# A retention state product on four 64x64 tiles of TensorE

## The chip, the cores and the metric

One core of a Trainium2 chip. The metric is the device time of one execution in microseconds; the verdict on a difference of 2% uses fast runs alone. The rounds ran on several chips, so each ratio is to the kernel before in the same rounds.

PE is TensorE, which multiplies matrices; DVE is VectorE, ACT is ScalarE, POOL is GpSimd; PEld is PE's loading of weights. PSUM is the memory that PE writes its products to. In the views, sps are the scores, ops the outputs (of the state product and of scores times values), xT the outputs times the decays, nps the tokens' product, ld the loaded q, k and v. A tile mode is the way in which the array is divided, as 64*64; a drain is here the time from the start of a group's last record to the start of the next group's first one in another mode.

## The reference, cut to what matters

Retention with a decay per head, then a mixture of experts in which each token runs one expert. The change lies in the first half; the second sees it only through the order of the 512 features.

```python
B, H, S, DH = 8, 8, 576, 64
gamma = 1.0 - 2.0 ** (-5.0 - arange(H))
ret = (q @ k.T / 8) * where(i >= j, gamma ** (i - j), 0)    # per head
x = (ret @ v) -> (B, S, H * DH)
# experts: fresh expert = argmax(x @ w_gate), kept from the token before where
# sigmoid(x @ w_local) >= 0.5; out = softmax prob * relu(x @ w1[e]) @ w2[e]
```

## The kernel before: the parts that matter

The 4608 tokens are cut into 36 chunks of 128. A sum of k-times-v per head (`kv`) carries the past from chunk to chunk. Two heads are stacked on the 128 partitions, so ACT copies `kv` into a block-diagonal `states`: head 2c in the upper left 64x64 block, head 2c+1 in the lower right, zeros elsewhere. One matmul then serves two heads.

```python
ps_s = pool(part, "ps_s", 3, PSUM)      # scores
ps_o = pool(part, "ps_o", 2, PSUM)      # outputs
ps_n = pool(part, "ps_n", 1, PSUM)      # outputs by token, two banks
ps_kv = pool(part, "ps_kv", 1, PSUM)
...
def outputs(i):                                          # cut
    ops = ps_o.tile([P, HP, P], F32, name="ops")
    if m > 0:                                            # the state product
        n = HALF if m == MID else P
        for c in range(HP):
            nc.tensor.matmul(ops[:, c, 0:n], lhsT=states[(i + 1) % 2][:, c, :], rhs=qT[:, c, 0:n], ...)
    if m != PER - 1:
        ...                                              # kv += k.T v, 8 matmuls on 128x64 tiles
        for u in range(2):
            nc.scalar.copy(states[i % 2][half(u), :, half(u)], kv[half(u)])
    for c in range(HP):                                  # scores times values, 128x64 tiles
        for u in range(2):
            nc.tensor.matmul(ops[half(u), c, :], lhsT=vs[...], rhs=sT[:, u, c, :], ...)
    nc.vector.tensor_tensor(xT, ops, decq[:, :, at:at + P], op=Alu.mult)
...
scores(0)
for i in range(NCH + 1):
    if i + 1 < NCH: scores(i + 1)        # 8 matmuls, 64x128 tiles
    if i < NCH: outputs(i)
    if i > 0: by_token(i - 1)            # 4 matmuls, whole array
```

A sequence has 576 tokens, so a pair of sequences is 9 chunks: the first has no past, the middle one (m = 4) ends one sequence and begins the next and streams only 64 columns in the state product.

## Time and profile before

| | before |
|---|---|
| median of the first three runs | 843.18 us |
| retention half, to the start of the last tokens' product | 177.70 us |
| one normal chunk on PE | 4.80 us |
| of it, state product to the start of kv | 1.09 us |

Two groups of the page's list of the costliest ones, the state product and the copies of the state. The columns are line, engine, operation, output and inputs, shapes and count, then busy time and mean ns of one, then idle time before.

```profile
L152 PE MATMUL ops<-ld,state 128*128 128x128 f32 (+1 forms) x256 | 36.7, 286 | 0.0
...
L167 ACT COPY state<-kv 64x256 f32<-64x256 f32 x64 | 23.5, 367 | 77.3 <-PE kv L162 76.5
```

The first has no idle time before it: PE goes from group to group. The second is on an engine that waits for PE. The 286 ns are the modelled length of one pipelined record, not its price: 36.7 us over 256 records is 143 ns.

### The profile page before, as it was taken

The numbers are of one execution on the slowest core, as the hardware profiler recorded it, in microseconds if no ns is written. First come the engines' busy times: TensorE is split into PE (matmuls) and PEld (weight loads), VectorE is DVE, ScalarE is ACT, GpSimd is POOL, SyncE is SP. The second block draws the span as 40 slices with busy tenths as digits, with TensorE's granted clock in tenths as the row PEclk, the third lists the DMA queues.
The fourth block names the chain that finished last, engine by engine and source line by source line (L and its number), as shares of the span: only waits on it lengthen the run. The fifth ranks groups of instructions, "written<-read, shape, count | busy, mean of one in ns | idle before, by whom it ended". The sixth has DMA issues, their size and how long they took to land.

```text
span 840.0 us, 10642 instructions
## 1 busy us (share of the span) xinstructions
PE 760.1 (90%) x4158; PEld 497.6 (59%) x4158; DVE 171.1 (20%) x314; ACT 99.8 (12%) x230; POOL 139.3 (17%) x157
## 2 busy tenths in 40 slices
PE   6999999951699999999799979998999999999991
PEld 5888888841556654754375456547544754565460
DVE  3444545458302021002101100210021011100000
ACT  1222222210011100110011001001100100011010
POOL 7322222210433021103101110210001001100000
PEclk9999999985799999999899999999999999999996
DMA  9788888616733321512420142213303301200000
GB/s 361 268 286 276 296 273 289 228 51 228 263 111 104 102 65 46 179 56 89 145 102 27 63 147 101 65 47 124 114 13 135 115 14 59 109 14 11 27 28 5
DMA packets 27649, 105.77 MB, mean 126 GB/s; under 512 B 4607, under 2 KB 4607, under 8 KB 22785
## 3 DMA queue, kind: packets, MB, share of 16 engines
q1 hardware_dynamic: 19584, 80.75, 27.6%
q0 software_dynamic: 7120, 22.03, 7.8%
q8 instruction: 71, 1.16, 0.6%
q10 hardware_dynamic: 816, 1.37, 0.4%
q14 instruction: 58, 0.47, 0.2%
HBM read 85.25 MB, written 20.19 MB: 126 GB/s over the span
## 4 chain that ended last, share of the span: by engine, by line
issue 49%; DMA 23%; PE 19%; POOL 4%; DVE 1%; POOLq 1%; SPq 0%; ACT 0%; ACTq 0%; another core or an unknown queue 0%; DVEq 0%
DMA out_dram<-y,sidx 19%; PE nps L183 5%; PE sps L133 4%; PE ops L152 4%; PE ops L171 4%; POOL xg L430 3%; DMA w2s<-in_w_dram 2%; PE kv L162 2%; DMA decq<-in_decay_q_dram 2%; POOL out_dram L470 0%; SPq L424 0%; POOLq L470 0%; POOLq L477 0%; POOLq L481 0%; ACT x L186 0%
## 5 line engine op out<-in xcount | busy, mean ns | idle before, releaser
L466 PE MATMUL yps<-w2s,hT 128*128 128x512 f32 x656 | 285.8, 593 | 0.6 <-PEq L477 0.6
L410 PE MATMUL hps<-xTs,w1s 128*128 128x384 f32 (+4 forms) x1024 | 265.5, 422 | 16.2 <-issue 15.3
L410 PEld LDWEIGHTS hps<-xTs,w1s 128*128 128x128 f32 x1024 | 189.3, 196 | 95.1 <-issue 26.1
L466 PEld LDWEIGHTS yps<-w2s,hT 128*128 128x128 f32 x656 | 123.5, 190 | 148.9 <-issue 147.4
L469 DVE TENSOR_SCALAR y<-yps,pslot 128x512 f32<-128x512 f32 x41 | 30.8, 751 | 465.9 <-PE yps L466 465.9
L412 ACT ACTIVATE hT<-hps 128x384 f32<-128x384 f32 (+4 forms) x128 | 53.5, 418 | 573.9 <-PE hps L410 515.2
L470 POOL DMA_INDIRECT out_dram<-y,sidx x41 | 40.8, 995 | 332.9 <-DVE y L469 290.5
L430 POOL DMA_INDIRECT xg<-xd,gidx x48 | 46.2, 962 | 223.0 <-PE xgps L435 169.0
L127 POOL TENSOR_TENSOR vs<-ld,deck 128x512 f32<-128x512 f32 x36 | 37.5, 1044 | 113.3 <-DMA ld<-in_qkv_dram 73.3
L133 PE MATMUL sps<-ld 64*128 64x128 f32 x576 | 44.4, 294 | 6.7 <-DMA ld<-in_qkv_dram 6.7
L137 DVE TENSOR_TENSOR sT<-sps,mask 128x512 f32<-128x512 f32 x72 | 46.4, 686 | 16.5 <-PE sps L133 16.5
L436 DVE COPY xTs<-xgps 128x512 f32<-128x512 f32 x48 | 31.6, 687 | 76.3 <-PE xgps L435 71.8
L183 PE MATMUL nps<-gates,xT 128*128 128x137 f32 x288 | 43.4, 292 | 1.1 <-DVE lt L187 0.9
L133 PEld LDWEIGHTS sps<-ld 64*128 64x128 f32 x576 | 37.3, 195 | 11.7 <-DMA ld<-in_qkv_dram 7.0
L435 PE MATMUL xgps<-ident,xg 128*128 128x128 f32 x192 | 30.8, 294 | 12.2 <-DMA xg<-xd,gidx 7.0
L183 PEld LDWEIGHTS nps<-gates,xT 128*128 128x128 f32 x288 | 36.1, 189 | 7.4 <-issue 5.3
L171 PE MATMUL ops<-sT,vs 128*64 128x128 f32 x576 | 38.9, 278 | 0.0
L435 PEld LDWEIGHTS xgps<-ident,xg 128*128 128x128 f32 x192 | 22.3, 147 | 25.8 <-issue 14.1
L152 PE MATMUL ops<-ld,state 128*128 128x128 f32 (+1 forms) x256 | 36.7, 286 | 0.0
L176 DVE TENSOR_TENSOR xT<-ops,decq 128x512 f32<-128x512 f32 x36 | 24.9, 691 | 44.9 <-PE ops L171 39.9
L152 PEld LDWEIGHTS ops<-ld,state 128*128 128x128 f32 x256 | 31.0, 191 | 3.8
L167 ACT COPY state<-kv 64x256 f32<-64x256 f32 x64 | 23.5, 367 | 77.3 <-PE kv L162 76.5
(121 smaller groups left out, 177.1 us busy)
## 6 DMA issues: line engine op xcount, KB each, us to landing
ld<-in_qkv_dram SPq DMA_DIRECT2D x36, 1024.0 KB, 6.9
w1s<-in_w_dram SPq DMA_DIRECT2D x32, 512.0 KB, 6.7
w2s<-in_w_dram SPq DMA_DIRECT2D x32, 512.0 KB, 7.9
xd<-x SPq DMA_DIRECT2D x36, 256.0 KB, 4.6
decq<-in_decay_q_dram ACTq DMA_DIRECT2D x1, 1280.0 KB
xg<-xd,gidx POOLq DMA_INDIRECT x48
out_dram<-y,sidx POOLq DMA_INDIRECT x41
deck<-in_decay_k_dram ACTq DMA_DIRECT2D x1, 36.0 KB
```

Of the source, the lines that this page charges most:

```text
L127: nc.gpsimd.tensor_tensor(vs.rearrange("p (h d) -> p h d", h=H), vn.rearrange("p (h d) -> p h d", h=H), deck[:, m, :].unsqueeze(2).to_broa ...
L133: nc.tensor.matmul(sps[u][:, c, :], lhsT=kT[half(u), c, :], rhs=qT[half(u), c, :], start=True, stop=True, skip_group_check=True)
L137: nc.vector.tensor_tensor(sT[:, u], sps[u], (mask2 if m == MID else mask).unsqueeze(1).to_broadcast([P, HP, P]), op=Alu.mult)
L152: nc.tensor.matmul(ops[:, c, 0:n], lhsT=states[(i + 1) % 2][:, c, :], rhs=qT[:, c, 0:n], start=(c == 0), stop=False, skip_group_check=True)
L171: nc.tensor.matmul(ops[half(u), c, :], lhsT=vs[:, h * DH:(h + 1) * DH], rhs=sT[:, u, c, :], start=(m == 0 and c == 0), stop=True, skip_gro ...
L183: nc.tensor.matmul(nps[:, c, 0:P + E + 1], lhsT=xT[:, c, :], rhs=gates[:, c, :], start=True, stop=True, skip_group_check=True)
L410: nc.tensor.matmul(hps[:, 0:n], lhsT=w1s[:, m, c, :], rhs=xT[:, c, base:base + n], start=(c == 0), stop=(c == DK - 1))
L412: nc.scalar.activation(hT[:, m, base:base + n], hps[:, 0:n], Act.Relu)
L430: nc.gpsimd.indirect_dma_start(out=xg, out_offset=None, in_=xd, in_offset=bass.IndirectOffsetOnAxis(ap=gidx[:, s:s + 1], axis=0))
L435: nc.tensor.transpose(xps[:, c, :], xg[:, c * P:(c + 1) * P], ident)
L466: nc.tensor.matmul(yps, lhsT=hT[:, m, u * P:(u + 1) * P], rhs=w2s[:, m, :], start=(m == 0), stop=(m == FK - 1))
L470: nc.gpsimd.indirect_dma_start(out=out, out_offset=bass.IndirectOffsetOnAxis(ap=sidx[:, s:s + 1], axis=0), in_=y, in_offset=None, bounds_c ...
```

## The change

Leave the zeros out: eight 64x64 matmuls (two row halves u times two column halves v of the array, twice) instead of four 128x128. So that all four tiles have work, each row half brings its output to both partition halves, and the heads come out in another order (`head_at`), and x's feature blocks are permuted; the host permutes the rows of the gates and of w1 alike. Row halves write different PSUM banks, so the outputs take two half-used banks, and the pool goes from two buffers to one.

```diff
+def head_at(k, u, v):
+    return 2 * (2 * k + (u ^ v)) + u
-        ps_o = pool(part, "ps_o", 2, PSUM)
+        ps_o = pool(part, "ps_o", 1, PSUM)
-        states = [once.tile([P, HP, P], F32, name=f"state{i}") for i in range(2)]
-        for t in states:
-            nc.vector.memset(t, 0.0)
+        states = [once.tile([P, HP, DH], F32, name=f"state{i}") for i in range(2)]
-            ops = ps_o.tile([P, HP, P], F32, name="ops")
+            ops = ps_o.tile([P, 2, 4 * P], F32, name="ops")
+            def place(k, u, v):
+                return ops[half(v), u, k * P:(k + 1) * P]
+            tiles = [(k, u, v) for k in range(HP // 2) for u in range(2) for v in range(2)]
-                for c in range(HP):
-                    nc.tensor.matmul(ops[:, c, 0:n], lhsT=states[(i + 1) % 2][:, c, :],
-                                     rhs=qT[:, c, 0:n], start=(c == 0), stop=False,
+                for k, u, v in tiles:
+                    c = head_at(k, u, v) // 2
+                    nc.tensor.matmul(place(k, u, v)[:, 0:n], lhsT=states[(i + 1) % 2][half(u), c, :],
+                                     rhs=qT[half(u), c, 0:n], start=(k == 0), stop=False,
-                for u in range(2):
-                    nc.scalar.copy(states[i % 2][half(u), :, half(u)], kv[half(u)])
+                nc.scalar.copy(states[i % 2], kv)
 ... (scores times values go over the same tiles; xT reads both banks;
      the decays, the gates and w1 are permuted on the host)
```

More of the change, by code (lines that the diff above doesn't have):

```diff
@@ L165, in outputs @@
                                          skip_group_check=True)
-                for u in range(2):
-                    nc.scalar.copy(states[i % 2][half(u), :, half(u)], kv[half(u)])
-            for c in range(HP):
-                for u in range(2):
-                    h = 2 * c + u
-                    nc.tensor.matmul(ops[half(u), c, :], lhsT=vs[:, h * DH:(h + 1) * DH],
-                                     rhs=sT[:, u, c, :], start=(m == 0 and c == 0), stop=True,
-                                     skip_group_check=True)
+                nc.scalar.copy(states[i % 2], kv)
+            for k, u, v in tiles:
+                h = head_at(k, u, v)
+                nc.tensor.matmul(place(k, u, v), lhsT=vs[:, h * DH:(h + 1) * DH],
+                                 rhs=sT[:, u, h // 2, :], start=(m == 0 and k == 0), stop=True,
+                                 skip_group_check=True)
             g["xT"] = xT = work.tile([P, HP, P], F32, name="xT")
             at = (m * P) % S
-            nc.vector.tensor_tensor(xT, ops, decq[:, :, at:at + P], op=Alu.mult)
+            nc.vector.tensor_tensor(
+                xT.rearrange("p (u k) s -> p u k s", u=2),
+                ops[:, :, 0:2 * P].rearrange("p u (k s) -> p u k s", k=2),
+                decq[:, :, at:at + P].rearrange("p (u k) s -> p u k s", u=2), op=Alu.mult)
         def by_token(i):
@@ L512, in _by_feature, with _heads @@
     return x.transpose(0, 3, 2, 1).reshape(NCH, P, D)
+def _heads(np):
+    return np.array([[head_at(k, u, v) for v in range(2)] for u in range(2) for k in range(HP // 2)])
 def _decays(np):
@@ L521, in _decays @@
     at = (np.arange(S + HALF) % S).astype(np.float64)
-    head = 2 * np.arange(HP)[None, :] + np.arange(P)[:, None] // DH
+    head = _heads(np)[None, :, :].repeat(DH, 0).transpose(2, 0, 1).reshape(P, HP)
     q = gamma[head][:, :, None] ** at / math.sqrt(DH)
@@ L534 @@
     i = {n: _np.asarray(a) for n, a in inputs.items()}
-    gates = _np.concatenate([i["moe_w_gate"], i["moe_w_local"]], 1)
+    order = (_heads(_np).reshape(H, 1) * DH + _np.arange(DH)).reshape(D)
+    gates = _np.concatenate([i["moe_w_gate"], i["moe_w_local"]], 1)[order]
     decay_k, decay_q = _decays(_np)
@@ L543 @@
         "wgl": gates.reshape(DK, P, E + 1).transpose(1, 0, 2).reshape(P, DK * (E + 1)),
-        "w1": i["moe_w1"].reshape(E, DK, P, FK, P).transpose(0, 2, 3, 1, 4).reshape(E, P, FK * D),
+        "w1": i["moe_w1"][:, order].reshape(E, DK, P, FK, P).transpose(0, 2, 3, 1, 4).reshape(E, P, FK * D),
         "w2": i["moe_w2"].reshape(E, FK, P, D).transpose(0, 2, 1, 3).reshape(E, P, FK * D),
```

## The prediction

> **What bounds the kernel now.** I read the page's slices first, then the busy times of two stretches, then one chunk in order of time, then the start, then single records where a merged line was too coarse. From the page, the slices:
>
> ```profile
> PE   6999999951699999999799979998999999999991
> PEclk9999999985799999999899999999999999999996
> DMA  9788888616733321512420142213303301200000
> ```
>
> One slice is 21 us. The retention half is the first eight slices and a bit, to about 178 us: PE full, its clock full, DMA high too. Then comes the routing (slices 8 to 10, PE half idle), then the experts, to 840. The diff touches the second and third parts only by permuting rows of the gates and of the first weights: same shapes, same counts, so I leave their 660 us as they are, and the question is what the 178 us become. The busy times of two stretches:
>
> ```profile
> 84.00:105.00 21.00, 21.00 (x268) 18.55 (x264) 10.50 (x20) 5.27 (x12) 5.06 (x5) 1.00 0.87 296
> 105.00:126.00 21.00, 21.00 (x291) 18.55 (x290) 9.08 (x17) 6.01 (x14) 4.34 (x5) 1.00 0.81 273
> ```
>
> PE is busy for all 21.00 us of both (columns: PE, weight loads, DVE, ACT, POOL, clock, DMA share, GB/s). DVE is at half, ACT and POOL at a quarter. DMA at 0.81 to 0.87 is the only other resource near its end. In the waits of 60 to 160 us no PE matmul waits for anything. So each chunk costs what its PE work costs. One chunk on PE, with DVE's product that reads the outputs:
>
> ```profile
> 106.57 1.21 PE L183 MATMUL nps<-gates,xT 128*128 128x137 f32 x8
> 107.70 1.16 PE L133 MATMUL sps<-ld 64*128 64x128 f32 x16
> 108.80 1.16 PE L152 MATMUL ops<-ld,state 128*128 128x128 f32 x8
> 109.88 0.69 PE L162 MATMUL kv<-vs,ld 128*64 128x64 f32 x16
> 110.40 1.04 PE L171 MATMUL ops<-sT,vs 128*64 128x128 f32 x16
> 111.37 0.38 PE L183 MATMUL nps<-gates,xT 128*128 128x137 f32 x1
> ...
> 106.69 0.69 DVE L176 TENSOR_TENSOR xT<-ops,decq 128x512 f32<-128x512 f32 x1 [1.31 <-PE ops L171]
> ```
>
> From start to start: tokens 1.13, scores 1.10, state product 1.08 to 1.09, kv 0.51 to 0.52, scores times values 0.97; sum 4.80 us per chunk. The state product is 23% of it, and half of what it multiplies is the zeros of the block-diagonal state. Each fp32 matmul leaves two records (four matmuls, x8). The start of the kernel:
>
> ```profile
> 15.32 1.16 PE L152 MATMUL ops<-ld,state 128*128 128x128 f32 x8
> 16.41 0.69 PE L162 MATMUL kv<-vs,ld 128*64 128x64 f32 x16
> 16.92 1.05 PE L171 MATMUL ops<-sT,vs 128*64 128x128 f32 x16
> 18.16 1.09 PE L183 MATMUL nps<-gates,xT 128*128 128x137 f32 x7 [0.19 <-DVE xT L176]
> ...
> 17.41 0.69 DVE L176 TENSOR_TENSOR xT<-ops,decq 128x512 f32<-128x512 f32 x1 [5.07 <-DMA decq<-in_decay_q_dram]
> ```
>
> The first xT waits 5.07 us for the decays' DMA. Meanwhile PE does all of chunk 1's outputs (15.32 to about 18.0), which it can because the outputs' PSUM tile has two buffers.
>
> **What the Trainium skill says.** (1) "TensorEngine Tiling (Array Packing)", Tiling Modes, Key Properties: tiles of one mode load weights and multiply in parallel; changing the mode drains the array. The trace agrees. Inside a two-tile group the records start in pairs 6.5 ns apart, one pair per 109 ns (scores times values, 64 columns of weights, 128 streamed) or 58 ns (kv, 64 streamed). From the last record of a group to the first of the next mode there are 201 to 205 ns (149 after 64 streamed columns); from kv to scores times values, one mode, there are only 52. (2) The same page, Restrictions and Gotchas, Gotcha 1: different row tiles must write different PSUM banks. That is why the new output tile spans two banks, half used, and has to give up its second buffer (3 + 2 + 2 + 1 banks = 8). (3) "TensorE: Matmul & The Clock Gate", LDWEIGHTS: the time of a weight load goes with its columns, not its rows. Agreed: after a drain the second load begins when the first stream ends (106 ns), and its matmul starts 107 ns later with 128 columns (state, scores), 54 ns later with 64 (kv and scores times values in the middle chunk, first gaps 107 and 160 ns).
>
> **The state product as it is.** Single records of one chunk: starts at 103.989 and 104.202 (first gap 213 ns), then 6 steps of 111.7, last at 104.872, and kv begins at 105.077 (drain 205): 213 + 670 + 205 = 1,088 ns.
>
> **The state product as it will be.** Eight matmuls 64x64, so 16 records, on four tiles, four per tile. In the order of the loop, four neighbours fall on four different tiles. If all four run together: first gap 160 (106 + 54, 64 columns of weights), two more steps of 109 (the two-tile pitch) = 218, stagger of the four about 20 (3 x 6.5), drain 204: about 602 ns. The mode changes on both sides stay two, as they are now. Saved: 1,088 - 602 = 486 ns.
>
> **The middle chunk of every pair of sequences** (4 chunks) streams only 64 columns: now 1.035 us (113.602 to 114.637, eight loads of 128 columns at 112 ns). New: first gap 107, two steps of 58, stagger 20 = 243, and then kv, which in this chunk is already in 64x64 tiles, follows with no drain, one step later (58) and without its own slow first gap (saves about 50). So about 0.30 - 0.05 = 0.25 us; saved 0.78.
>
> **The other parts.** Scores times values keep 16 records, alternate column halves as before, only the heads are in another order: 0. ACT's two copies of 64x256 (0.37 us each) become one of 128x256: ACT gains 0.37 us per chunk, but it already ends 2.2 us before the next state product: 0. The two memsets of the states (DVE, at 1.0 us) go: 0, nothing waited. The xT product reads 512 elements per partition as before, out of two banks: 0.69 us still.
>
> **The lost buffer.** The next outputs may start only when xT has read the last ones. In the steady state xT starts 0.12 us after the tokens' matmuls begin and takes 0.69, so it ends at +0.81; the next state product starts at +2.22 (1.13 + 1.10). Slack 1.4 us: no wait. At the start it does cost: chunk 1's state product must wait for xT of chunk 0, which ends at 18.10, so state, kv and scores times values (0.60 + 0.52 + 0.97 = 2.09) come after 18.15, and the first tokens' product moves from 18.16 to about 20.24. Loss 2.1 us, once; chunk 1's own saving is in that number.
>
> **Sum.** 36 chunks; 4 first ones have no state, chunk 1 is counted in the loss, 4 are middle ones, so 27 normal ones remain. 27 x 0.486 = 13.1; 4 x 0.78 = 3.1; minus 2.1: 14.1 us. 843.2 - 14.1 = 829.1 us, 1.7% less. A normal chunk becomes 4.80 - 0.49 = 4.31 us.
>
> **Rivals.**
> - DMA takes over. A chunk moves 1.00 MB in and 0.25 MB out, 1.31 million bytes. The two stretches gave 296/0.87 = 340 and 273/0.81 = 337 GB/s per full share, so a chunk can't take under about 3.9 us (estimate). At 4.31 us the share would be 0.93 on average. For it: that is close, and 2-KB packets of the stores mix in. Against it: a load issued at 101.04 landed at 108.10 and its scores ran at 112.51, 4.4 us later; with shorter chunks some 3.5 us are left. If landing slipped behind PE all the same, chunks of 4.5 us would leave 6 to 8 us of gain: 835 to 837. I give it one in ten.
> - The four tiles don't run four at a time, only two. Then 8 pairs: 160 + 6 x 109 + 204 + 10, about 1.03 us, no gain in the normal chunk, and the start's loss stays: 842 to 845. Against it: row pairs (scores) and column pairs (the values' product) both run together in this trace[...]. At 8.77 to 9.36 us, when one row tile waited for a PSUM buffer, three records of the other tile ran ahead of it, so a tile doesn't hold up its neighbour. One in fifteen.
> - The start loses nothing, because the instructions are scheduled otherwise (kv of chunk 1 needs no output buffer and could go into the wait): up to 2 us more gain, 827.
> - The lost buffer stalls every chunk. The slack of 1.4 us speaks against it; if the stall ate half of the saving, 836. Unlikely.
> - Finer overlap of four tiles, with a pitch of 100 instead of 109 or a shorter first gap: 30 to 50 ns per chunk, 1 to 1.5 us, 828.
>
> **Range and chances.** The centre is 829.1. The threshold of 2% is 826.3: it takes a group of about 0.52 us or less with the loss as told, or both a free start and a slightly faster group: 10%. Slower by over 2% needs a stall that I don't see: 1%. The rest, 89%, lies within 2%. Range of eight in ten: 826 to 834, wider upwards for DMA and for part-way concurrency.
>
> **What would show it.** In the changed profile: the state product's group with x16 records of 64*64, 0.60 us from its start to kv's; starts in fours some 6.5 ns apart; the chunk's period 4.31 us; DMA share in the stretches 0.90 to 0.95 with PE still at 21.00 of 21.00; the first tokens' product at 20.2 us, after an idle time of nearly 2.9 us ended by DVE's xT; the routing and the experts shifted by 14 us and not otherwise changed. Wrong would be: starts in twos, PE idle before the scores (loads late), PE idle before each state product (buffer), or an expert half that itself changes its time, of which nothing here speaks.

## The result, and the profile after

The changed kernel took 831.53 us (median of 4, 830.27 to 832.81), the kernel before 843.79 in the same session (median of 4). The ratio is 0.9855, 95% interval 0.9833 to 0.9876: 1.5% less, within 2%. Ratios here are the mean time of one kernel's fast runs over that of the other's in the same rounds, so not quite the ratio of the medians. The predicted 829.1 was 2.4 us too low, inside its range.

The slices of the page after (one is 20.7 us here):

```profile
PEclk9999999957799999999899989998999999999996
DMA  8899999419632122420422142233103302200000
```

DMA is now at nine tenths in the retention half. Two stretches of it (columns as before):

```profile
63.00:84.00 21.00, 21.00 (x356) 18.11 (x353) 10.51 (x21) 4.79 (x10) 5.16 (x6) 1.00 0.91 309
84.00:105.00 21.00, 21.00 (x346) 18.18 (x344) 11.28 (x21) 4.51 (x10) 5.60 (x6) 1.00 0.96 326
```

PE is still busy for all 21.00 us: DMA at 0.91 to 0.96 has not yet become the bound. One normal chunk and the first half of a middle one, PE in order of time:

```profile
103.53 0.67 PE L163 MATMUL ops<-ld,state 64*64 64x128 f32 x16
104.13 0.69 PE L173 MATMUL kv<-vs,ld 128*64 128x64 f32 x16
104.64 1.04 PE L180 MATMUL ops<-sT,vs 128*64 128x128 f32 x16
105.62 1.21 PE L195 MATMUL nps<-gates,xT 128*128 128x137 f32 x8
106.75 1.16 PE L137 MATMUL sps<-ld 64*128 64x128 f32 x16
107.84 0.46 PE L163 MATMUL ops<-ld,state 64*64 64x64 f32 x16
108.14 0.63 PE L173 MATMUL kv<-vs,ld 64*64 64x64 f32 x16
```

Read the starts: the state product has 0.60 us to kv's start where it had 1.09, and 0.30 us in the middle chunk, where it had 1.035. From state product to state product (103.53 to 107.84) a chunk takes 4.31 us. The single records of the first group start at 103.528, .535, .541, .548, then at .688, .797 and .906 for the next fours: four at a time, 6.5 ns apart, first gap 160, steps of 109. Now the start:

```profile
17.29 0.69 DVE L185 TENSOR_TENSOR xT<-ops,decq 128x512 f32<-128x512 f32 x1 [5.07 <-DMA decq<-in_decay_q_dram]
...
18.13 0.67 PE L163 MATMUL ops<-ld,state 64*64 64x128 f32 x16 [3.78 <-DVE xT L185]
...
18.73 0.84 PE L173 MATMUL kv<-vs,ld 128*64 128x64 f32 x16
...
19.35 1.92 PE L180 MATMUL ops<-sT,vs 128*64 128x128 f32 x16
...
21.20 1.83 PE L195 MATMUL nps<-gates,xT 128*128 128x137 f32 x8
```

PE waits 3.78 us for DVE's xT, as the lost buffer makes it. And then scores times values (19.35 to 21.20) take 1.85 us, not 0.97, and the tokens (21.20 to 22.96) 1.76, not 1.13. The trace's clock records say why: from 19.10 to 22.51 us PE was granted half its clock. The kernel before had a full clock from 14.4 us to the end of its retention half. So the start cost 3.04 us up to the tokens' product (18.16 to 21.20) and 0.63 in it: 3.7 us where 2.1 were expected.

From the first tokens' product to the last, 159.54 us became 143.97, that is 15.6 us less; with the 0.6 us of the slow clock taken out, 16.2, the sum of the prediction's two terms (13.1 + 3.1). The retention half ends 12.5 us earlier (177.70 to 165.17). Routing and experts together took 662.3 us before and 663.4 after. In all kernels they took 661.2 to 667.4 us, scattered over kernels whose second half is the same.

### The profile page after: what moved, and what is told of

It reads as the page before. It is cut to its first block, busy times and chain, and to the rows that moved or that the text cites. A ratio compares the mean times of both kernels' runs of the same rounds, so it can differ in the third digit from the quotient of the medians.

```text
span 828.6 us, 11144 instructions
## 1 busy us (share of the span) xinstructions
PE 744.2 (90%) x4414; PEld 481.3 (58%) x4414; DVE 170.1 (21%) x312; ACT 88.2 (11%) x198; POOL 139.4 (17%) x157
## 4 chain that ended last, share of the span: by engine, by line
issue 47%; DMA 24%; PE 21%; POOL 2%; DVE 2%; POOLq 1%; SPq 0%; ACT 0%; ACTq 0%; DVEq 0%
DMA out_dram<-y,sidx 20%; PE nps L195 5%; PE sps L137 4%; PE ops L180 4%; PE hps L422 3%; DMA w2s<-in_w_dram 2%; PE kv L173 2%; PE ops L163 2%; DMA decq<-in_decay_q_dram 2%; POOL xg L442 2%; PE xgps L447 1%; DMA xg<-xd,gidx 0%; PE yps L478 0%; SPq L436 0%; POOLq L482 0%
## 5 line engine op out<-in xcount | busy, mean ns | idle before, releaser
L137 PEld LDWEIGHTS sps<-ld 64*128 64x128 f32 x576 | 37.1, 195 | 11.4 <-DMA ld<-in_qkv_dram 6.9
L180 PEld LDWEIGHTS ops<-sT,vs 128*64 128x64 f32 x576 | 31.7, 140 | 1.0 <-issue 0.7
L198 ACT COPY x<-nps 128x512 f32<-128x512 f32 x36 | 21.1, 586 | 64.9 <-PE nps L195 64.9
L393 PE MATMUL slots<-col,row 128*128 128x156 f32 x72 | 11.4, 326 | 17.1 <-DVE col L384 17.1
```

The lines of the kernel that those rows point to most:

```text
L137: nc.tensor.matmul(sps[u][:, c, :], lhsT=kT[half(u), c, :], rhs=qT[half(u), c, :], start=True, stop=True, skip_group_check=True)
L180: nc.tensor.matmul(place(k, u, v), lhsT=vs[:, h * DH:(h + 1) * DH], rhs=sT[:, u, h // 2, :], start=(m == 0 and k == 0), stop=True, skip_gr ...
```

## The experiments

All ten gave correct results.

**1. Keep PE busy in the wait.** Is it the idle time that costs the clock? Thirteen matmuls without use go into the free tokens' tile ahead of chunk 1's outputs.

```diff
+            if i == 1:
+                warm = ps_n.tile([P, DK, 2 * P], F32, name="warm", tag="n")
+                for c in range(13):
+                    nc.tensor.matmul(warm[:, c % DK, 0:P], lhsT=gates[:, c % DK, 0:P], rhs=gates[:, 0, 0:P], ...)
```

> The changed kernel with 13 idle-time matmuls into the free tokens' PSUM tile, placed between chunk 2's scores and chunk 1's state product, about 2.9 us of work in the 3.8 us in which PE waits for the first xT. The wait itself stays. Theory 'the idle PE loses its clock': no half-clock stretch after 19 us, chunk 1's kv and scores times values at 0.52 and 0.98 us instead of 0.62 and 1.85, first tokens' product at 20.2 us instead of 21.2, end of the retention half 1.6 us earlier than in the changed kernel (last tokens' product at about 163.6 instead of 165.2). Rival 'the slow stretch has another cause (loads, PSUM)': it stays, first tokens' product at 21.2 or later.

PE at the start:

```profile
15.34 3.17 PE L211 MATMUL warm<-gates 128*128 128x128 f32 x26
18.55 0.67 PE L164 MATMUL ops<-ld,state 64*64 64x128 f32 x16
19.15 0.69 PE L174 MATMUL kv<-vs,ld 128*64 128x64 f32 x16
19.66 1.04 PE L181 MATMUL ops<-sT,vs 128*64 128x128 f32 x16
20.64 1.21 PE L196 MATMUL nps<-gates,xT 128*128 128x137 f32 x8
...
17.71 0.69 DVE L186 TENSOR_TENSOR xT<-ops,decq 128x512 f32<-128x512 f32 x1 [5.38 <-DMA decq<-in_decay_q_dram]
```

828.42 us, ratio 0.9823 (0.9802 to 0.9843). No half clock from 14.4 us to the end of the half; kv at 0.51 us, scores times values at 0.98. Useless work shortened the retention half; that the whole kernel got quicker is less sure, since this interval overlaps the changed kernel's. The tokens' product came at 20.64, not 20.2, because in this run the decays landed later: xT began at 17.71 us instead of 17.29, and the state product started 0.15 us after its end, as in the changed kernel. So the half ends 1.2 us earlier (163.98), not 1.6. The Trainium skill, "TensorE: Matmul & The Clock Gate", Part 1, says the clock halves after an idle window of some 3.4 us that runs freely against the kernel; the traces agree on the halving, and it lasted one such window in the changed kernel (3.4 us) and two in run 5 (6.8 us). They don't show that the idle time must be that long (runs 2 and 10). The rival, slow loads or PSUM, fell.

**2. The kernel before, with one output buffer.** Does the lost buffer cost anything beyond the start?

```diff
-        ps_o = pool(part, "ps_o", 2, PSUM)
+        ps_o = pool(part, "ps_o", 1, PSUM)
```

> The kernel before with one buffer for the outputs' PSUM tile instead of two, nothing else. Theory: only the start loses. First tokens' product from 18.16 to 20.7 us (xT of chunk 0 ends at 18.1, then 1.09 + 0.52 + 0.97), so +2.6 us, and +1.6 more if the idle time trips the clock as it did in the changed kernel; chunk period still 4.80 us; total 1.003 to 1.005 of the kernel before. Rival 'the lost buffer stalls every chunk a little': period above 4.80, total over 1.01.

```profile
18.24 2.05 PE L152 MATMUL ops<-ld,state 128*128 128x128 f32 x8 [2.80 <-DVE xT L176]
20.21 1.12 PE L162 MATMUL kv<-vs,ld 128*64 128x64 f32 x16
21.12 1.15 PE L171 MATMUL ops<-sT,vs 128*64 128x128 f32 x16
22.20 1.21 PE L183 MATMUL nps<-gates,xT 128*128 128x137 f32 x8
```

849.19 us, ratio 1.0064 (1.0043 to 1.0084). The tokens' product moved from 18.16 to 22.20 us, and the retention half ends 4.04 us later (181.74): the same 4.0. So after the start nothing was lost: from the first tokens' product to the last it is 159.54 us in both. An idle time of 2.80 us was enough to halve the clock (17.9 to 21.3 us). The rest of the 5.5 us lies in the second half, 665.9 us in this profile. The ratio is a little above the 1.003 to 1.005 that I expected; that scatter of the second half is the likely reason, not a shown one.

**3 and 4. First decays early.** If the wait for the decays is the price of the lost buffer, then loading 256 KB of them first should give it back in the changed kernel, and next to nothing in the kernel before, which hid it.

```diff
+        decq0 = once.tile([P, HP, P], F32, name="decq0")
+        nc.scalar.dma_start(out=decq0, in_=decay_q.rearrange("p (c s) -> p c s", c=HP)[:, :, 0:P])
 ...
+            dq = decq0 if at == 0 else decq[:, :, at:at + P]
```

> The changed kernel with the first 128 columns of the query decays loaded by a small DMA of their own (256 KB) ahead of the rest, so that xT of the first chunk need not wait for 1.28 MB. Theory: the start's wait was the price of the lost buffer; xT of chunk 0 begins at about 13.5 us, chunk 1's state product right after chunk 2's scores at about 14.4, first tokens' product at about 16.5 instead of 21.2 us, no half clock; the retention half ends 4 to 5 us earlier than in the changed kernel, total about 827 us, ratio to the kernel before about 0.980. Rival 'the loads bound the start anyway': scores of chunks 3 to 5 wait for their loads and the end gains under 2 us.

> The same early load of the first decays in the kernel before. With two output buffers the wait for the decays was hidden behind chunk 1's outputs but for some 0.2 us, so the theory says 0.2 to 0.5 us gained, ratio 0.999 to 1.000. Rival 'the late decays cost both kernels alike': 3 us or more gained here too.

PE in the changed kernel with early decays:

```profile
15.55 0.67 PE L165 MATMUL ops<-ld,state 64*64 64x128 f32 x16 [0.27 <-DVE xT L188]
...
17.64 1.21 PE L198 MATMUL nps<-gates,xT 128*128 128x137 f32 x8
```

Changed kernel: 827.95 us, ratio 0.981 (0.9787 to 0.9832). The wait shrank to 0.27 us, the tokens' product came at 17.64, the half ends at 160.98, 4.2 us earlier. I had expected the tokens' product at 16.5: the 256 KB landed later than I thought, so xT began at 14.71 us, not 13.5. Routing and experts took 666.3 us in this profile, long for this study, so the total gained less than 4.2 us; against 2% the verdict is unclear. Kernel before: 843.24, ratio 0.9992 (0.997 to 1.0014), tokens' product at 18.04: 0.1 us gained, where I had told 0.2 to 0.5. The late decays cost only the kernel with one buffer.

**5. The loop over the tiles turned round.** Must neighbours in the loop fall on different tiles?

```diff
-            tiles = [(k, u, v) for k in range(HP // 2) for u in range(2) for v in range(2)]
+            tiles = [(k, u, v) for u in range(2) for v in range(2) for k in range(HP // 2)]
```

> The changed kernel with the loop over the tiles turned round: both matmuls of one quadrant first, then the next quadrant, in the state product and in scores times values. Theory 'each tile takes its matmuls from a common queue and later ones may pass those of another tile that is busy': state product still 0.60 to 0.70 us, starts still in fours, chunk period 4.31 to 4.45, ratio to the kernel before 0.985 to 0.990. Rival 'matmuls start in program order, so only neighbours overlap': state product about 4 x (160 + 218) + 204 ns = 1.7 us, scores times values slower too, ratio above 1.03.

```profile
101.78 0.69 PE L163 MATMUL ops<-ld,state 64*64 64x128 f32 x16
102.39 0.69 PE L173 MATMUL kv<-vs,ld 128*64 128x64 f32 x16
102.91 1.10 PE L180 MATMUL ops<-sT,vs 128*64 128x128 f32 x16
103.94 1.21 PE L195 MATMUL nps<-gates,xT 128*128 128x137 f32 x8
```

832.06 us, ratio 0.9859 (0.9831 to 0.9886). The state product takes 0.62 us, starts still come in fours, now 13 ns apart; scores times values take 1.03 instead of 0.98 us. Order is worth 0.07 us per chunk (medians 4.387 and 4.316), not a factor: the rival is out. The start of this run cost more than in the others: after an idle time of 3.10 us the half clock lasted 6.8 us (17.3 to 24.1), and the tokens' product came at 22.28 us. Whether the array lets matmuls of different tiles pass each other, or they are put in another order on the way to it, this trace can't tell.

**6. Two column tiles, zeros kept.** How much comes from smaller weight loads and the saved mode change, without leaving out the zeros? The kernel before, with the state product on 128x64 tiles.

```diff
-                    nc.tensor.matmul(ops[:, c, 0:n], lhsT=states[(i + 1) % 2][:, c, :],
-                                     rhs=qT[:, c, 0:n], ...)
+                    for v in range(2):
+                        nc.tensor.matmul(ops[half(v), c, 0:n], lhsT=states[(i + 1) % 2][:, c, half(v)],
+                                         rhs=qT[:, c, 0:n], ...)
```

> The kernel before with the state product on two column tiles (128 rows x 64 columns, zeros still multiplied, two output buffers and one bank kept). Rival to be tested: 'what the change saved came from smaller weight loads and from the mode change (drain), not from leaving out the zeros'. Worked out from the trace: 160 + 6 x 109 + 109 = 0.92 us from the state product's start to kv's, no drain before kv and kv's first gap gone (0.05), so 0.21 us per chunk saved against 0.49 with four tiles; 28 x 0.21 + 4 x 0.43 = 7.6 us in all, ratio about 0.991. If zeros are what costs, it stays at that part; if loads and drains were all, it would come near the changed kernel's 0.985.

```profile
100.37 1.09 PE L153 MATMUL ops<-ld,state 128*64 128x128 f32 x16
101.29 0.63 PE L163 MATMUL kv<-vs,ld 128*64 128x64 f32 x16
101.76 1.05 PE L172 MATMUL ops<-sT,vs 128*64 128x128 f32 x16
```

836.33 us, ratio 0.9921 (0.9894 to 0.9947). 0.92 us to kv's start, and kv 0.47 instead of 0.51: as worked out. So 0.2 us of a chunk can be had by smaller weight loads and a shared mode, with two buffers kept and no permutation. The change's 0.49 us is more than that, and it pays for two mode changes like the kernel before. By the single records, 53 ns of it are the shorter first gap (213 to 160), and 432 the six steps that became two and a stagger (670 to 238 ns): most of its gain is the zeros left out.

**7 to 9. Sharing modes.** If a mode change costs a drain and a slow first gap, scores on 64x64 tiles should join the state product, and the tokens' product on 128x64 tiles should join kv and scores times values. All three start from the changed kernel with early decays: scores only, both, tokens only.

```diff
-                    nc.tensor.matmul(sps[u][:, c, :], lhsT=kT[half(u), c, :], rhs=qT[half(u), c, :], ...)
+                    for v in range(2):
+                        nc.tensor.matmul(sps[u][half(v), c, :], lhsT=kT[half(u), c, half(v)],
+                                         rhs=qT[half(u), c, :], ...)
-                nc.tensor.matmul(nps[:, c, 0:P + E + 1], lhsT=xT[:, c, :], rhs=gates[:, c, :], ...)
+                for v in range(2):
+                    nc.tensor.matmul(nps[half(v), c, 0:P + E + 1], lhsT=xT[:, c, half(v)], rhs=gates[:, c, :], ...)
```

> The changed kernel with early first decays, and the scores too on four 64x64 tiles (16 matmuls with 64 columns of weights instead of 8 with 128), so that scores and state product share a mode. Theory (drain plus slow first gap are paid per mode change): scores plus state product from 1.09 + 0.60 = 1.69 us to 160 + 6 x 109 + 109 + 3 x 109 + 20 + 204 = 1.47 us; period 4.31 to 4.09 us; 7 us less than with early decays alone, about 821 us, ratio 0.973. Rival 'DMA is the bound now': a chunk's 1.31 MB at 338 GB/s takes 3.9 us, so loads start to come late, PE idles before the scores, period stays above 4.2.

> As scores64, and the tokens' matmuls on two column tiles, so that kv, scores times values and tokens share a mode too: two mode changes per chunk instead of four. PE alone would need about 0.2 us less again: 3.9 us per chunk, which is the estimate of DMA's own 3.9. Theory: DMA becomes the bound here; PE idles before the scores for loads, period 3.95 to 4.1, DMA share 0.95 or more, ratio 0.967 to 0.973. Rival 'DMA still has room': period 3.9, no idle PE, ratio about 0.966.

> The changed kernel with early first decays and only the tokens' matmuls on two column tiles (8 matmuls with 64 columns of weights instead of 4 with 128), so that kv, scores times values and tokens share a mode; scores stay as they are. Theory 'each mode change costs its drain and a slow first gap': period 4.31 - 0.2 = about 4.1 us, about 7 us less than with early decays alone, ratio 0.973 to 0.976, as for the scores on four tiles. It also tells apart what stopped the version with both: if it was the number of PE instructions to be fetched, this one (40 matmuls per chunk against 44 and 48) has no idle PE; if it was DMA's share alone, idle spots appear at the same period as there.

Scores only: 822.35 us, ratio 0.9755 (0.9729 to 0.9781). Scores and state product from 104.20 to 105.67 us, 1.47 as expected; a normal chunk 4.10. The ratio told was 0.973.

Both: 824.99 us, ratio 0.976 (0.9715 to 0.9806), no better. Undisturbed chunks take 3.91 us, but PE stops now and then where it waits for nothing that the profile shows, in the middle of a group:

```profile
92.28 0.88 PE L140 MATMUL sps<-ld 64*64 64x128 f32 x22
93.63 0.48 PE L140 MATMUL sps<-ld 64*64 64x128 f32 x9 [0.47 <-issue]
```

Between 30 and 140 us there are six such stops, idle for 0.5 to 1.5 us each and 6.4 in all. The loads of ld are not what it waits for, so my theory of late loads fell. The last record before each stop starts 0.6 to 1.9 us after a fetch on the instruction queue q8 did, which would fit a PE that ran out of instructions; but 13 of that queue's 19 fetches were followed by no stop.

Tokens only: 819.87 us, ratio 0.973 (0.9712 to 0.9747), the lowest of all ratios here (its interval overlaps that of scores only), over 2% faster than the kernel before. PE:

```profile
104.45 1.04 PE L182 MATMUL ops<-sT,vs 128*64 128x128 f32 x16
105.33 1.11 PE L199 MATMUL nps<-gates,xT 128*64 128x137 f32 x16
106.37 1.16 PE L139 MATMUL sps<-ld 64*128 64x128 f32 x16
```

Scores times values give way to the tokens after 0.88 us, not 0.98, and the tokens take 1.04, not 1.13; a normal chunk 4.12 us. DMA's share in its stretches is 0.94 to 0.96 (where both were done, 0.85 to 0.96), and between 30 and 140 us PE never idles. So DMA's share as such doesn't stop PE. Scores only, with 44 matmuls per chunk between the 40 here and the 48 of both, had one stop in that time, idle for 0.6 us. That the instructions are what stops PE is argued, not shown: the more matmuls, the shorter the period was too.

**10. The changed kernel again**, in the same rounds as tokens only:

> The changed kernel itself, unaltered, for comparison in the same rounds on the same chip: 0.985 to 0.987 of the kernel before; chunk period 4.31 to 4.32 us, a half-clock stretch of 3.4 us in the first 25 us.

830.00 us, ratio 0.9853 (0.9831 to 0.9875); retention half to 165.33 us, a normal chunk 4.32, half clock from 19.0 for 3.4 us, here after an idle time of 2.30 us by the profile. The 0.9855 stands. Against it in the same rounds, tokens only is 0.973 / 0.9853 = 0.988.

## Why the prediction was right, point by point

- **The bound.** PE set the retention half, before and after: right (21.00 of 21.00 us busy in the stretches).
- **The state product on four tiles.** 602 ns told, 598 measured, by the very steps: four starts at once, 160, twice 109, a drain of 200. The rival of two at a time is out. The middle chunk: 0.78 saved told; from the state product to scores times values 1.65 us became 0.86, so 0.79.
- **What should give nothing gave nothing.** One copy of the state instead of two, the memsets gone: no row on the path changed. Scores times values in the new order: 0.98 us.
- **The lost buffer.** No wait in the steady state: right, shown by the kernel before with one buffer. The loss at the start was the right mechanism with too small a size, and this is the term that was mis-sized: "Loss 2.1 us, once". It measured 3.7 us. I had added the work that moves behind the wait at full speed, and left out that PE's clock is halved for 3.4 us around and after such a wait. Filling the wait removed that stretch. The wait itself was 3.78 us for nearly 2.9 told, and 2.30 in run 10: PE reached it earlier or later as its clock rose at 12.3 or 15.6 us.
- **DMA.** Share 0.91 and 0.96 for 0.93 told, loads landing in 7.5 us instead of 6.9 (medians), no idle PE: the rival stayed away, and even at 4.12 us per chunk it did.
- **The start scheduled otherwise.** Did not happen: kv stayed behind the state product.
- **The end.** Retention half 12.5 us shorter for 14.1 told; the difference is the 1.6 us of the clock. The rest of the program scatters by more than that from profile to profile, so end-to-end medians of 12 us and single profiles of 11.4 are one result.
- **A slip that cost nothing.** By the prediction's own sum, 2% would have needed a state product of 0.50 us, not 0.52.

## What to carry to other kernels

Count a PE group as first gap, steps and drain, each read from single records, and a tile change can be worked out to within a few ns; neighbours that share a tile mode save the drain, which here was worth 0.2 us per chunk where the change brought 0.49. When a change gives up a buffer, look for the one place where it hid a wait, usually the start, and load first what that wait is for. And the four runs here in which PE sat idle for 2.30 to 3.78 us at the start paid more than the wait: half the clock for 3.4 to 6.8 us.

## What the Trainium skill lacked or had wrong

- "TensorEngine Tiling (Array Packing)", Key Properties, says that a mode change drains but not what it costs. Here, with fp32 and 128 streamed columns, 199 to 205 ns from the last record to the next mode's first instead of a step of 109, and then a first gap of 160 ns (64 weight columns) or 213 (128) instead of 109 to 112.
- "TensorE: Matmul & The Clock Gate", Part 1, speaks of idle windows of about 3.4 us. Idle times of 2.80 and 2.30 us by the profile came with a half-clock stretch of 3.4 us as well, and one of 3.10 with 6.8 us, so shorter waits aren't safe. Idle times here are read from modelled ends of matmuls.
- The same page, Part 3, calls matmuls strict FIFO in start and end. With all matmuls of a quadrant next to each other in the program, starts still came in fours 13 ns apart and the group took 0.62 us; in strict program order the first four starts would lie on one tile, where a step takes 109 ns. Something between program and array lets tiles pass each other; which, the runs don't show.
- No page gives a measured time of an fp32 matmul in a stream (there are a count of passes and a peak rate): here two records per matmul, each 109 to 112 ns for 128 columns and 58 for 64.
